# A convolution with two expert layers: folds in pairs, a clamp moved to ScalarE, a spectrum computed earlier, tiles of 512

## The chip, the cores and the metric

The kernel runs on one core of one Trainium2 chip. The metric is the device time of one execution in microseconds. A core has five engines with instruction queues of their own: TensorE multiplies matrices (PE; its weight loads are listed apart as PEld), VectorE (DVE), ScalarE (ACT) and GpSimd (POOL) work element by element, and SyncE (SP) here only issues DMA transfers. ScalarE issues some DMAs too.

## The reference

```python
window = np.exp(-0.01 * np.arange(S))[:, None]                      # S = 12480
h_filt = (np.maximum(pos_emb @ w1, 0) @ w2) * window                # 12480 x 128
u = x * v
y = irfft(rfft(u, 2 * S) * rfft(h_filt, 2 * S), 2 * S)[:S]          # along the sequence
t = x * y                                                           # 12480 tokens x 128
h = t @ moe_w_in;   t = (h * clip(h + 3, 0, 6) / 6) @ moe_w_out     # 128 -> 2048 -> 128
h = t @ moe2_w_in;  out = where(h > 0, h, exp(min(h, 0)) - 1) @ moe2_w_out
```

Everything is fp32, but the four weight matrices of the expert layers arrive as fp64.

## The kernel before, in words

The convolution is a Fourier transform of 196 x 128 points, factored: a first stage of products over 98 rows for each channel, a second over 128 columns for each of 99 frequencies, then back in a third and a fourth. It runs once for the filter and for the signal, and the signal's second stage goes over two halves of 64 channels.

*MLP (`filter_hidden`, L264 to L278).* Eight rounds of eight position products (L267) go to PSUM; VectorE applies relu and window (L271), and the fold (L275 to L278) writes the sum and the difference of two halves to `Rf`. VectorE makes the sums, GpSimd the differences of the first six rounds, VectorE those of the last two. Between rounds stand two calls of `signal` (L254 to L261), three GpSimd operations that make four channels of u = x * v and its own fold. The channel is the outer dimension of `Rf` and the position the inner one, while the data come with the channel inside.

*First stage (L295 to L308).* 32 steps; a step makes eight products (L299; the trace counts two passes of each) for four channels, of the filter or of the signal, and ScalarE copies the result (L302).

*Second stage (`second_all`, L376 to L402).* Its first half goes through 27 groups of up to four frequencies, two groups a turn. For a turn, TensorE makes the filter's spectrum (`second_r`, L324), ScalarE copies it (L327); then come the signal's products (L316) and the filter's last ones (L331). In `second`, ScalarE copies the latter (`ta`, L336), VectorE makes two complex products from them (`tb` and `tc`, L338) and GpSimd combines these (L344). The second half needs no spectrum of its own and goes group by group. The third stage (L353 to L363) stands between the two halves, mixed with the other half's first stage (L420 to L427), and the fourth (L461) makes the tokens.

*Weights (`weight_steps`, L149 to L186).* All through these stages VectorE turns the fp64 weights into fp32 by integer operations, in 32 jobs of 128 x 256 numbers with three steps each. Step one takes the exponent (L174) and the mantissa's upper bits (L175) and clamps the exponent to 896..1151 (L176); step two adds the lower bits (L178), moves the exponent to its place (L179), stores the job before (a DMA on ScalarE's queue, L164) and loads the one after next (SP's queue, L159); step three puts sign and exponent together (L183) and scales (L184). `convert(n)` pays out steps by a rate: 1.1 per step of the first stage, 1.5 per group in the second stage's first half up to frequency 72 (18 groups, so one job in each of nine turns), 1.5 in the third stage, 0.6 per group in the second half.

*Expert layers (L528 to L640).* The tokens go in 26 tiles of `TT` = 480. A tile takes eight units in each of the two layers, and a unit twelve products, six into the hidden layer (L575, `mm1`) and six out of it (L619, `mm2`), since each factor is split into two parts. 26 x 16 x 12 = 4992 products.

No scheduler reorders anything: each engine runs in the order in which the code issues, and the four PSUM buffers of `ps` are shared by all convolution stages.

## Time and profile before

| | us |
|---|---|
| median of three runs | 1441.62 (1440.79 to 1445.14) |
| profiled execution, its own time | 1442.68 |
| its span in the trace | 1440.9 |
| TensorE busy | 1407.4 (98%) |
| VectorE busy | 1235.1 (86%) |
| ScalarE busy | 990.4 (69%) |
| GpSimd busy | 519.8 (36%) |

A span is the time from the first instruction to the last; the execution's own time is 1.8 us longer. The expert layers take 346.00 to 1437.30, three quarters of the span. Busy shares are means over stages that differ, so the rows further down are cut by stage. Where a row ends in square brackets, it says how long the engine had been idle before, and what ended that.

### The profile page before, as it was taken

The numbers are of one execution on the slowest core, as the hardware profiler recorded it, in microseconds if no ns is written. First come the engines' busy times: TensorE is split into PE (matmuls) and PEld (weight loads), VectorE is DVE, ScalarE is ACT, GpSimd is POOL, SyncE is SP. The second block draws the span as 40 slices with busy tenths as digits, with TensorE's granted clock in tenths as the row PEclk, the third lists the DMA queues.
The fourth block names the chain that finished last, engine by engine and source line by source line (L and its number), as shares of the span: only waits on it lengthen the run. The fifth ranks groups of instructions, "written<-read, shape, count | busy, mean of one in ns | idle before, by whom it ended". The sixth has DMA issues, their size and how long they took to land.

```text
span 1440.9 us, 21903 instructions
## 1 busy us (share of the span) xinstructions
PE 1407.4 (98%) x8414; PEld 1229.8 (85%) x8414; DVE 1235.1 (86%) x1401; ACT 990.4 (69%) x1168; POOL 519.8 (36%) x438
## 2 busy tenths in 40 slices
PE   7999999999999999999999999999999999999998
PEld 5888879898888888888888888888888888888887
DVE  7999669788898888888888888888888888888887
ACT  0533332356887877777777777777777777787776
POOL 7855987411332222222222222222222222222223
PEclk9999999999999999999999999999999999999999
DMA  5854355136000000000000000000000000000000
GB/s 186 260 162 139 95 164 150 46 102 182 1 1 7 8 7 7 8 8 0 8 7 7 8 8 7 1 8 7 8 7 8 8 7 1 8 8 8 8 7 14
DMA packets 36660, 60.74 MB, mean 42 GB/s; under 512 B 4290, under 2 KB 17996, under 8 KB 36428
## 3 DMA queue, kind: packets, MB, share of 16 engines
q1 hardware_dynamic: 31436, 54.68, 12.5%
q10 hardware_dynamic: 5120, 4.66, 1.0%
q8 instruction: 66, 1.08, 0.3%
q14 instruction: 38, 0.31, 0.1%
HBM read 48.74 MB, written 10.58 MB: 41 GB/s over the span
## 4 chain that ended last, share of the span: by engine, by line
PE 80%; DVE 12%; POOL 3%; issue 2%; ACT 1%; DMA 1%; SPq 0%; DVEq 0%; POOLq 0%; ACTq 0%
PE h L575 37%; PE o L619 37%; PE y L461 3%; PE q L353 3%; DVE tb L338 2%; DVE tc L338 1%; DVE qb L178 1%; POOL au L344 1%; DVE qb L176 1%; POOL late L260 1%; DVE qb L183 1%; DVE qb L276 1%; POOL ld L257 1%; DVE qb L179 1%; DVE qb L174 1%
## 5 line engine op out<-in xcount | busy, mean ns | idle before, releaser
L619 PE MATMUL o<-gs,w 128*128 128x480 f32 x2496 | 579.5, 380 | 0.2 <-DVE gs L609 0.2
L588 POOL TENSOR_SCALAR a<-a 128x960 f32<-128x960 f32 x208 | 288.1, 1385 | 743.9 <-ACT a L587 703.1
L619 PEld LDWEIGHTS o<-gs,w 128*128 128x128 f32 x2496 | 469.2, 188 | 74.6 <-DVE gs L609 0.6
L609 DVE TENSOR_TENSOR gs<-g,gs 128x960 fp32r<-128x960 f32 x416 | 485.7, 1168 | 4.4 <-ACT gs L604 4.4
L604 ACT CAST gs<-g 128x960 fp32r<-128x960 f32 x416 | 412.6, 992 | 56.4 <-DVE g L596 54.7
L596 DVE SCALAR_TENSOR_TENSOR g<-a,h 128x960 f32<-128x960 f32 x208 | 240.0, 1154 | 140.4 <-ACT a L585 140.3
L575 PE MATMUL h<-xs,w 128*128 128x480 f32 x1248 | 306.2, 381 | 3.0 <-POOL w L490 1.9
L575 PE MATMUL h<-x,w 128*128 128x480 f32 x1248 | 304.1, 379 | 0.0
L575 PEld LDWEIGHTS h<-xs,w 128*128 128x128 f32 x1248 | 234.9, 189 | 40.6 <-POOL w L490 2.3
L587 ACT ACTIVATE a<-h 128x960 f32<-128x960 f32 x208 | 202.4, 973 | 94.4 <-PE h L575 93.5
L575 PEld LDWEIGHTS h<-x,w 128*128 128x128 f32 x1248 | 234.1, 188 | 38.2 <-issue 0.4
L585 ACT ACTIVATE a<-h,three 128x960 f32<-128x960 f32 x208 | 220.9, 1062 | 63.2 <-PE h L575 62.8
L598 DVE SCALAR_TENSOR_TENSOR g<-a,h 128x960 f32<-128x960 f32 x208 | 238.5, 1147 | 0.2 <-POOL a L588 0.2
L344 POOL TENSOR_TENSOR au<-tb,tc 128x256 f32<-128x256 f32 (+3 forms) x108 | 90.2, 868 | 45.4 <-DVE tc L338 44.2
L336 ACT COPY ta<-z 128x512 f32<-128x512 f32 (+3 forms) x54 | 29.7, 550 | 62.1 <-DVE tc L338 25.8
L353 PEld LDWEIGHTS q<-cs,au 128*99 128x99 f32 x512 | 56.6, 170 | 7.2 <-issue 4.6
L353 PE MATMUL q<-cs,au 128*99 128x128 f32 x512 | 60.0, 275 | 2.8 <-POOL au L344 1.8
L490 POOL TENSOR_TENSOR w<-w 128x512 fp32r<-128x512 f32 x16 | 24.6, 1541 | 103.7 <-ACT w L489 60.7
L331 PE MATMUL z<-qb 128*128 128x128 f32 x396 | 53.3, 283 | 4.2 <-ACT qb L327 4.2
L299 PE MATMUL pa<-t,qb 98*64 98x198 f32 x512 | 51.2, 356 | 6.3 <-POOL qb L259 3.7
L359 DVE TENSOR_TENSOR qb<-q,tb 99x512 f32<-99x512 f32 (+2 forms) x68 | 41.4, 654 | 17.9 <-ACT tb L357 17.7
L299 PEld LDWEIGHTS pa<-t,qb 98*64 98x64 f32 x512 | 40.0, 147 | 17.2 <-POOL qb L259 4.4
(56 smaller groups left out, 967.6 us busy)
## 6 DMA issues: line engine op xcount, KB each, us to landing
ld<-in_xc SPq DMA_DIRECT2D x32, 196.0 KB
qb<-in_vc SPq DMA_DIRECT2D x32, 196.0 KB
out_T<-y SPq DMA_DIRECT2D x26, 240.0 KB
xt<-in_xT SPq DMA_DIRECT2D x31, 195.0 KB
qb<-in_mw SPq DMA_DIRECT2D x22, 256.0 KB
qb<-in_gm SPq DMA_DIRECT2D x22, 256.0 KB
...
```

Of the source, the lines that this page charges most:

```text
L299: nc.tensor.matmul(pa[f * HN:(f + 1) * HN, j, :2 * NK], lhsT=src[:, j, f], rhs=t1[:, f], start=True, stop=True)
L344: nc.gpsimd.tensor_tensor(out=Au[:, slots(hf), k0:k0 + nk, r], in0=m1[:, :, :nk, r], in1=m2[:, :, :nk, 1 - r], op=op)
L353: nc.tensor.matmul(q[:NK, r, j], lhsT=Au[:, s0 + j, :, r], rhs=cs[:, r * N2:(r + 1) * N2], start=True, stop=True)
L575: nc.tensor.matmul(h[:, j, :TT], lhsT=wslice(2 * m - 2, a, 2 * u + j), rhs=x[:, b], start=i == 0, stop=i == 2)
L585: nc.scalar.activation(a, h[:, :, :TT], AF.Relu, bias=three)
L587: nc.scalar.activation(a, h[:, :, :TT], AF.Exp)
L588: nc.gpsimd.tensor_scalar(a, a, 1.0, 0.0, op0=ALU.min, op1=ALU.max)
L596: nc.vector.scalar_tensor_tensor(g, a, 6.0, h[:, :, :TT], op0=ALU.min, op1=ALU.mult)
L598: nc.vector.scalar_tensor_tensor(g, a, -1.0, h[:, :, :TT], op0=ALU.add, op1=ALU.max)
L604: nc.scalar.copy(t[:, 0], g)
L609: nc.vector.tensor_tensor(out=t[:, 1], in0=g, in1=t[:, 0].bitcast(F32), op=ALU.subtract)
L619: nc.tensor.matmul(o[:, :TT], lhsT=wslice(2 * m - 1, a, 2 * u + j), rhs=gs[:, b, j], start=u == 0 and j == 0 and i == 0, stop=u == NU - 1 ...
```

## The change

Four edits, with the line numbers of the changed kernel.

The fold (L283) writes `Rf` with two neighbouring channels innermost, so that an output runs over pairs; the first stage's weights are then read with a stride of two (L308).

The clamp of the exponents leaves VectorE. Two ScalarE activations (L184, L185), both relu with an operand of one number per partition from a small tile `ramps`, do the clamp and the shift of the exponent together: relu(1151 - e) and then relu(255 - that), both scaled by 2^23. They are issued at the start of step two, ahead of that step's store.

`second_all` calls `second_r` one turn ahead: `rows(0)` before the loop, and in each turn the spectrum of the next.

`TT` becomes 512: 24 tiles of 512 tokens and one of 192, so 25 x 192 = 4800 products.

```diff
-TT = 480
-NT = S // TT
+TT = 512
+TILES = [slice(t, min(t + TT, S)) for t in range(0, S, TT)]
+NT = len(TILES)
+WID = [t.stop - t.start for t in TILES]
...
-    Rf = qb[:H1, HP:HP + FO * N2].rearrange("p (f s i) -> p f s i", f=FO, s=2)
+    Rf = qb[:H1, HP:HP + FO * N2].rearrange("p (g s i t) -> p s i g t", s=2, i=HN, t=2)
...
+        ramps = const.tile([128, 2], F32, name="ramps")
+        v.memset(ramps[:, :1], 1151 * 2.0 ** 23)
+        v.memset(ramps[:, 1:], 255 * 2.0 ** 23)
...
             v.tensor_scalar(ri, hi_w, 0xFFFFF, 0x100000, op0=ALU.bitwise_and, op1=ALU.bitwise_or)
-            v.tensor_scalar(ei, ei, 896, 1151, op0=ALU.max, op1=ALU.min)
             yield
+            nc.scalar.activation(e, ei, AF.Relu, bias=ramps[:, :1], scale=-(2.0 ** 23))
+            nc.scalar.activation(ei, e, AF.Relu, bias=ramps[:, 1:], scale=-1.0)
             v.scalar_tensor_tensor(r, lo_w, 2.0 ** -32, ri, op0=ALU.mult, op1=ALU.add)
-            v.tensor_scalar(ei, ei, -896, 2 ** 23, op0=ALU.add, op1=ALU.mult)
             store(k - 1)
             load(k + 2)
...
             e.tensor_tensor(
-                out=Rf[:, :, s, i0:i0 + GI].rearrange("p f i -> p i f"), in0=t[:, :, 0], in1=t[:, :, 1], op=op
+                out=Rf[:, s, i0:i0 + GI], op=op, **{
+                    f"in{x}": t[:, :, x].rearrange("p i (g t) -> p i g t", t=2) for x in range(2)
+                },
             )
...
-        first(Rf[:, c * DC:(c + 1) * DC], Ar[:, c * DC:(c + 1) * DC])
+        first(lambda j, f: Rf[:, f, :, c * DC // 2 + j // 2, j % 2], Ar[:, c * DC:(c + 1) * DC])
...
+        def rows(n):
+            if hf == 0 and n <= TAIL:
+                second_r(n, size(n) if n < TAIL else len(KGROUPS) - TAIL)
+        rows(0)
         while n < len(KGROUPS):
...
+            rows(n + size(n))
             g = [
...
-            if hf == 0 and n <= TAIL:
-                second_r(n, len(g) if n < TAIL else len(KGROUPS) - TAIL)
...
-                    h[:, j, :TT], lhsT=wslice(2 * m - 2, a, 2 * u + j), rhs=x[:, b], start=i == 0, stop=i == 2
+                    h[:, j], lhsT=wslice(2 * m - 2, a, 2 * u + j), rhs=x[:, b], start=i == 0, stop=i == 2
```

ScalarE's order in the second stage's first half, before (L336 copies `ta` for both groups of a turn, L164 stores a converted job, L327 copies the spectrum):

```order
L336 COPY ta<-z 128x512 x2
L164 DMA w_scratch<-qb 128x256
L327 COPY qb<-r 128x1024
L336 COPY ta<-z 128x512 x2
L164 DMA w_scratch<-qb 128x256
```

and the same stretch now (L345 is `ta`, L184 and L185 are the ramps, L170 the store, L336 the spectrum's copy):

```order
L345 COPY ta<-z 128x512 x2
L184 ACTIVATE qb<-qb,ramps 128x256
L185 ACTIVATE qb<-qb,ramps 128x256
L170 DMA w_scratch<-qb 128x256
L336 COPY qb<-r 128x1024
L345 COPY ta<-z 128x512 x2
```

The two ramps stand between the `ta` copies of one turn and the store; the store and the spectrum's copy, now that of the turn after, come behind them.

VectorE's order there, before (L338 makes `tb` and `tc`, L174 to L184 are one job):

```order
L338 TENSOR_TENSOR tb<-z,ta 128x4x64x2
L338 TENSOR_TENSOR tc<-z,ta 128x4x64x2
L174 TENSOR_SCALAR qb<-late 128x256
L175 TENSOR_SCALAR qb<-late 128x256
L176 TENSOR_SCALAR qb<-qb 128x256
L178 SCALAR_TENSOR_TENSOR qb<-late,qb 128x256
L179 TENSOR_SCALAR qb<-qb 128x256
L338 TENSOR_TENSOR tb<-z,ta 128x4x64x2
L338 TENSOR_TENSOR tc<-z,ta 128x4x64x2
L183 SCALAR_TENSOR_TENSOR qb<-late,qb 128x256
```

and now (L347 makes `tb` and `tc`):

```order
L347 TENSOR_TENSOR tb<-z,ta 128x4x64x2
L347 TENSOR_TENSOR tc<-z,ta 128x4x64x2
L180 TENSOR_SCALAR qb<-late 128x256
L181 TENSOR_SCALAR qb<-late 128x256
L186 SCALAR_TENSOR_TENSOR qb<-late,qb 128x256
L347 TENSOR_TENSOR tb<-z,ta 128x4x64x2
L347 TENSOR_TENSOR tc<-z,ta 128x4x64x2
L190 SCALAR_TENSOR_TENSOR qb<-late,qb 128x256
L191 SCALAR_TENSOR_TENSOR qb<-qb 128x256
```

Two operations of the job are gone; the exponent operation, which the ramps read, still stands behind the products of the turn's second group.

TensorE's order at the start of the second stage, before (`r` is the spectrum, `z` the products of L316 and L331; x8 counts products, two passes each):

```order
L299 MATMUL pa<-t_91,qb 64x198 x256
L324 MATMUL r<-qb 128x128 x8
L316 MATMUL z<-au,qb 128x128 x8
L331 MATMUL z<-qb 128x128 x8
L324 MATMUL r<-qb 128x128 x8
```

and now:

```order
L308 MATMUL pa<-t_91,qb 64x198 x256
L333 MATMUL r<-qb 128x128 x16
L325 MATMUL z<-au,qb 128x128 x8
L340 MATMUL z<-qb 128x128 x8
L333 MATMUL r<-qb 128x128 x8
```

Two turns' spectra stand ahead of the first turn's products, and afterwards each turn's products stand behind the spectrum of the next.

## Rows read from the trace of the kernel before

**Rows 1.** The page's chain that ended last, share of the span by engine
```profile
PE 80%; DVE 12%; POOL 3%; issue 2%; ACT 1%; DMA 1%; SPq 0%; DVEq 0%; POOLq 0%; ACTq 0%
```

**Rows 2.** Stretches: us; busy (instructions) per engine, PE to POOL; PEclk, DMA share, GB/s
```profile
32.40:80.60 48.20, 45.85 (x478) 36.84 (x478) 47.17 (x72) 22.90 (x29) 40.13 (x40) 0.93 0.79 233
80.60:160.90 80.30, 73.08 (x628) 70.30 (x627) 68.67 (x132) 30.71 (x45) 50.76 (x60) 1.00 0.41 125
160.90:213.50 52.60, 50.76 (x448) 41.40 (x448) 40.05 (x82) 18.86 (x27) 49.95 (x43) 1.00 0.50 155
213.50:270.50 57.00, 52.66 (x430) 50.67 (x429) 47.30 (x77) 16.11 (x29) 44.01 (x54) 0.97 0.45 130
40.00:60.00 20.00, 20.00 (x240) 16.67 (x236) 19.52 (x31) 10.06 (x13) 15.18 (x17) 1.00 0.99 296
```

**Rows 3.** Timeline of PE, end of the MLP: start, us, instruction, [idle before <-releaser]
```profile
28.99 3.13 PE L299 MATMUL pa<-t,qb 98*64 98x198 f32 x16 [0.81 <-POOL qb L260]
...
32.50 3.90 PE L299 MATMUL pa<-t,qb 98*64 98x198 f32 x22 [0.38 <-DVE qb L276]
```

**Rows 4.** Timeline of DVE, folds of the MLP
```profile
14.46 1.05 DVE L276 TENSOR_TENSOR qb<-au 98x512 f32<-98x512 f32 x1
...
29.55 2.90 DVE L276 TENSOR_TENSOR qb<-au 98x512 f32<-98x512 f32 x2
```

**Rows 5.** Timeline of POOL, folds of the MLP and the second signal
```profile
19.77 5.22 POOL L276 TENSOR_TENSOR qb<-au 98x512 f32<-98x512 f32 x3
24.94 1.26 POOL L257 TENSOR_TENSOR ld<-ld,qb 98x512 f32<-98x512 f32 x1
```

**Rows 6.** Groups by line: xcount | busy us, mean ns | idle before
```profile
L359 DVE TENSOR_TENSOR qb<-q,tb 99x512 f32<-99x512 f32 (+2 forms) x68 | 41.4, 654 | 17.9 <-ACT tb L357 17.7
...
L176 DVE TENSOR_SCALAR qb<-qb 128x256 int32<-128x256 int32 x32 | 22.8, 711 | 0.0
...
L179 DVE TENSOR_SCALAR qb<-qb 128x256 int32<-128x256 int32 x32 | 16.3, 511 | 0.0
```

**Rows 7.** Timeline of DVE, one turn of the second stage's first half
```profile
114.80 0.28 DVE L174 TENSOR_SCALAR qb<-qb 128x256 int32<-128x256 int32 x1
...
117.25 0.68 DVE L338 TENSOR_TENSOR tb<-z,ta 128x512 f32<-128x512 f32 x1
...
120.97 0.28 DVE L174 TENSOR_SCALAR qb<-late 128x256 int32<-128x256 int32 x1
```

**Rows 8.** Timeline of ACT and its DMA queue in that turn
```profile
113.71 0.36 ACTq L164 DMA_DIRECT2D w_scratch<-qb  x1
114.11 1.01 ACT L327 COPY qb<-r 128x1024 f32<-128x1024 f32 x1 [2.38 <-PE z L316]
116.42 0.59 ACT L336 COPY ta<-z 128x512 f32<-128x512 f32 x1 [1.30 <-PE z L331]
```

**Rows 9.** Timeline of PE in that turn
```profile
115.17 2.05 PE L331 MATMUL z<-qb 128*128 128x128 f32 x16 [0.50 <-ACT qb L327]
117.06 1.95 PE L324 MATMUL r<-qb 128*128 128x128 f32 x16
```

**Rows 10.** Groups of ACT by line and shape
```profile
L370 ACT ACTIVATE tmp<-pa,pm 99x196 f32<-99x196 f32 x65 | 26.3, 452 | 16.7 <-DVE ti L371 16.7
...
L336 ACT COPY ta<-z 128x256 f32<-128x256 f32 x4 | 1.5, 372 | 4.5 <-DVE tc L338 4.5
```

**Rows 11.** Timeline of POOL, signals in the third stage
```profile
165.65 0.73 POOL L259 TENSOR_TENSOR late<-ld 98x256 f32<-98x256 f32 x1
...
191.62 2.27 POOL L260 TENSOR_TENSOR late<-ld 98x256 f32<-98x256 f32 x1
```

**Rows 12.** Timeline of DVE, five groups of the second stage's second half
```profile
219.96 0.68 DVE L338 TENSOR_TENSOR tb<-z,ta 128x512 f32<-128x512 f32 x1
...
230.88 0.67 DVE L338 TENSOR_TENSOR tb<-z,ta 128x512 f32<-128x512 f32 x1
```

**Rows 13.** Stretch of the expert layers, PE alone: us, busy (x), PEclk, DMA
```profile
480.00:1408.00 928.00, 928.00 (x4267) 1.00 0.02 7
```

More of the change, by code (lines that the diff above doesn't have):

```diff
@@ L299, in first @@
                 nc.tensor.matmul(
-                    pa[f * HN:(f + 1) * HN, j, :2 * NK], lhsT=src[:, j, f], rhs=t1[:, f], start=True, stop=True
+                    pa[f * HN:(f + 1) * HN, j, :2 * NK], lhsT=src(j, f), rhs=t1[:, f], start=True, stop=True
                 )
@@ L304, in first_u @@
     def first_u(ut, slot):
-        first(ut, Au[:, slot:slot + DC])
+        first(lambda j, f: ut[:, j, f], Au[:, slot:slot + DC])
     def first_r(c):
-        first(Rf[:, c * DC:(c + 1) * DC], Ar[:, c * DC:(c + 1) * DC])
+        first(lambda j, f: Rf[:, f, :, c * DC // 2 + j // 2, j % 2], Ar[:, c * DC:(c + 1) * DC])
     def slots(hf):
@@ L377, in second_all, with size @@
         n = 0
+        def size(n):
+            return min(2 if n == 0 or hf == 0 and n != TAIL - 1 else 1, len(KGROUPS) - n)
+        def rows(n):
+            if hf == 0 and n <= TAIL:
+                second_r(n, size(n) if n < TAIL else len(KGROUPS) - TAIL)
+        rows(0)
         while n < len(KGROUPS):
@@ L381, in second_all @@
                     us.append(signal(*take()))
+            rows(n + size(n))
             g = [
                 (ps.tile([128, 2, KC, 2 * HD], F32, tag="ps", name="z"), take() if hf else gms[(n + i) % len(gms)], *k)
-                for i, k in enumerate(KGROUPS[n:n + (2 if n == 0 or hf == 0 and n != TAIL - 1 else 1)])
+                for i, k in enumerate(KGROUPS[n:n + size(n)])
             ]
-            if hf == 0 and n <= TAIL:
-                second_r(n, len(g) if n < TAIL else len(KGROUPS) - TAIL)
             early = hf == 1 and n == 0
@@ L534, in split @@
         x = xs[t % 2] if m == 1 else sb.tile([128, 2, TT], F32R, tag=f"x{m}", name=f"x{m}", bufs=2)
+        x = x[:, :, :WID[t]]
         nc.scalar.copy(x[:, 0], src)
@@ L542, in load_x @@
         if t < NT:
-            split(n, 1, t, xp[:, t * TT:(t + 1) * TT])
+            split(n, 1, t, xp[:, TILES[t]])
     def leave(n, m, t):
-        y = sb.tile([128, TT], F32, tag=f"y{m}", name=f"y{m}")
+        y = sb.tile([128, TT], F32, tag=f"y{m}", name=f"y{m}")[:, :WID[t]]
         if m == 1:
-            nc.scalar.mul(y, acc[m][:, :TT], 1.0 / 6.0)
+            nc.scalar.mul(y, acc[m][:, :WID[t]], 1.0 / 6.0)
             split(n, 2, t, y)
         else:
-            nc.scalar.copy(y, acc[m][:, :TT])
-            nc.sync.dma_start(outT[:, t * TT:(t + 1) * TT], y)
+            nc.scalar.copy(y, acc[m][:, :WID[t]])
+            nc.sync.dma_start(outT[:, TILES[t]], y)
     units = []
@@ L570, in mm1 @@
         m, t, u = units[n]
-        h = pp.tile([128, 2, 512], F32, tag="h", name="h")
+        h = pp.tile([128, 2, 512], F32, tag="h", name="h")[:, :, :WID[t]]
         x = xin[m, t]
@@ L582, in act1 @@
         h = st[n][0]
-        a = sb.tile([128, 2, TT], F32, tag="a", name="a", bufs=3)
+        a = sb.tile([128, 2, TT], F32, tag="a", name="a", bufs=3)[:, :, :WID[units[n][1]]]
         if m == 1:
-            nc.scalar.activation(a, h[:, :, :TT], AF.Relu, bias=three)
+            nc.scalar.activation(a, h, AF.Relu, bias=three)
         else:
-            nc.scalar.activation(a, h[:, :, :TT], AF.Exp)
+            nc.scalar.activation(a, h, AF.Exp)
             nc.gpsimd.tensor_scalar(a, a, 1.0, 0.0, op0=ALU.min, op1=ALU.max)
@@ L593, in gate @@
         h, a = st[n]
-        g = sb.tile([128, 2, TT], F32, tag="g", name="g", bufs=3)
+        g = sb.tile([128, 2, TT], F32, tag="g", name="g", bufs=3)[:, :, :WID[units[n][1]]]
         if m == 1:
-            nc.vector.scalar_tensor_tensor(g, a, 6.0, h[:, :, :TT], op0=ALU.min, op1=ALU.mult)
+            nc.vector.scalar_tensor_tensor(g, a, 6.0, h, op0=ALU.min, op1=ALU.mult)
         else:
-            nc.vector.scalar_tensor_tensor(g, a, -1.0, h[:, :, :TT], op0=ALU.add, op1=ALU.max)
+            nc.vector.scalar_tensor_tensor(g, a, -1.0, h, op0=ALU.add, op1=ALU.max)
         st[n] = [g]
@@ L602, in hi @@
         g = st[n][0]
-        t = sb.tile([128, 2, 2, TT], F32R, tag="gs", name="gs", bufs=LAG + 1)
+        t = sb.tile([128, 2, 2, TT], F32R, tag="gs", name="gs", bufs=LAG + 1)[:, :, :, :WID[units[n][1]]]
         nc.scalar.copy(t[:, 0], g)
```

2 lines of the change are left out of this document (1 added, 1 removed).

## The prediction

> **What bounds the kernel now.** I read the chain of waits first, since it says which engine's time is the kernel's time: 80% of it is TensorE, 12% VectorE, 3% GpSimd, 1% ScalarE [rows 1]. Those 12% and 3% all lie before the mixture-of-experts layers, so I next cut the span into stages [rows 2]: the filter's MLP up to 32.40 us, the first transform stage to 80.60, the second stage's first half to 160.90, the third stage with the other half's first stage to 213.50, the second stage's second half to 270.50. In the first stage VectorE is busy 47.17 of 48.20 us; in the next TensorE (73.08 of 80.30) and VectorE (68.67) take turns in waiting; in the third GpSimd is the fullest engine besides TensorE, 49.95 of 52.60. The profiled execution took 1442.68 us with a span of 1440.9, 1.06 above the median of 1441.62; sums are made against it, and 1.06 taken off at the end.
>
> **(a) Fold of the MLP.** VectorE's last two folds end at 29.55 + 2.90 = 32.45, and TensorE's first product on the filter, at 32.50, waited only 0.38 for them: until then it worked on the second signal's step, from 28.99 for 3.13, and that waited for GpSimd's signal [rows 3, 4]. So two chains end there, and both must shorten. On VectorE a fold took 1.05 alone, two at the end 2.90, 1.45 each [rows 4]; on GpSimd three in a row 5.22, 1.74 each [rows 5]. A fold writes down a column of strides; after the change its innermost output is two neighbours. The nearest operation that writes such pairs is L359, 512 elements in 654 ns [rows 6]. VectorE's ten folds then save 0.4 to 0.8 each and are done by 26.5 or so. GpSimd has six folds ahead of the second signal; at 1.74 less 0.6 or so, VectorE's own saving halfway, they save 3.6, and the signal's step starts at about 25.3. The step and the wait behind it follow: −3.8. Bounds: −1.2 if GpSimd's fold saves only 0.2, −6 if both chains close up on VectorE's 26.5. The stride of two in the weights of the first-stage products I cost at nothing; TensorE loads weights beside its products, and has 36.84 us of loads in 48.20 [rows 2].
>
> The Trainium skill ("SBUF — State Buffer", section "SBUF: two separate sides") says that VectorE and GpSimd share a port pair under an exclusive lock, which VectorE takes for operations with two inputs in SBUF, and that the other one blocks. The rows agree: 1.45 for a fold beside GpSimd's, 1.05 alone [rows 4]. By it a shorter fold on one engine gives the other its time back too, and (a) would come to −6 and the whole to 1433.5.
>
> **(b) First stage, 48.20 us.** Two operations of a conversion job leave VectorE: the clamp (711 ns) and the exponent's step (511 ns), 1.22 of a job's seven operations; VectorE averages 47.17 / 72 = 0.655, so seven are 4.6 us [rows 2, 6]. They return as two ScalarE ramps, which nothing replaces on VectorE but which the job's last two operations await. A job becomes about 3.9: 3.4 left on VectorE, and about 0.5 of waiting for the ramps that the mantissa's operations don't cover. But TensorE is close behind: in 40 to 60 us it is 20.00 of 20.00 busy, 240 instructions at 16 a step, so 1.33 a step, and the DMA engines are at 0.99 and 296 GB/s [rows 2]. The stage's 72 operations are 10.3 jobs, 40 us for VectorE at 3.9. TensorE's 30 steps on from 32.50 took 1.60 each; at 1.33 they would save 8. As GpSimd (40.13 busy) and the DMA stand close behind I take 1.43, 30 x 0.17 = −5. Bounds: −8 to +6 (the ramps stand behind copies, second rival).
>
> **(c) Second stage, first half: the step that decides.** There are nine turns of two channel groups with one job step each. One turn is 120.97 − 114.80 = 6.17, from exponent operation to exponent operation, and VectorE's products and job operations follow one another in it [rows 7]; over the stage it is 68.67 of 80.30 busy. TensorE waits 0.50 in it for the copy of the filter's spectrum [rows 9]: that wait goes, as the spectrum is now a turn ahead, but it isn't what sets the turn. What does afterwards is the order of ScalarE's queue. Before, a turn is: copy of the second group, store (0.36), spectrum copy (1.01), copy of the next turn's first group (0.59) [rows 8]. Now two ramps stand between that copy and the store, and they wait for the exponent operation, which VectorE reaches only behind the two products of the second group. Everything behind the ramps on ScalarE waits too: the store, the spectrum copy and the next turn's first copy, for which VectorE's next products wait. So a ring: exponent operation 0.28, 0.04 to the ramp, 0.48 + 0.02 + 0.48, 0.04, store 0.36 and 0.04, spectrum copy 1.01, copy 0.59 and 0.03, in all 3.37; then VectorE from its first product at 117.25 to the next exponent operation at 120.97, 3.72 [rows 7]. Less a few hundredths of overlap, 7.0 a turn in place of 6.17: 9 x 0.84 = +7.6.
>
> The ramp's price: 256 elements without an operand per partition took 372 ns, 196 elements with one 452 [rows 10]; the latter at 0.85 ns an element (0.59 for 512 [rows 8], against 372) would be 503 for 256. I take 0.48, nearest to the row with the operand; the ends move a turn by −0.22 and +0.04.
>
> The Trainium skill ("ScalarE: Activation LUTs", section "Rules for kernel authors") says that relu, max, min, add and multiply belong on VectorE, not on ScalarE: it speaks against this edit. By its figure for an activation with an operand per partition (section "What ACT_TABLE_LOAD costs", 280 ns and 0.833 per element) a ramp would be 0.49 and the turn by an estimate 7.02; the trace has no ramp yet to compare.
>
> Ahead of the loop a turn's spectrum is now computed before anything can cover it: 16 more products, 1.95 as in [rows 9], of which the end of the first stage hides a part, +1.2. Together +8.8. Bounds: −4 (first rival) to +10.5 (ramps at 0.5 and nothing of the start hidden). The turns behind the last conversion are unchanged but for the layout of waits; nothing.
>
> **(d) Third stage.** Here GpSimd is fullest, 49.95 of 52.60 with 43 operations [rows 2]. A signal undisturbed is 1.26 + 0.73 + 0.73, and one subtraction took 2.27 in place of 0.73 [rows 5, 11]. Fourteen signals at 2.72 would be 38.1, so 11.8 are stalls; two of the seven VectorE operations of a job that get in GpSimd's way go, 2/7 of that, 3.3; I take −3. Bounds: 0 (TensorE, 50.76 busy, holds the stage) to −4.
>
> **(e) Second stage, second half.** Five groups took 230.88 − 219.96 = 10.92 with one job in them [rows 12]. The two operations that leave (1.22) shorten VectorE's share, and here the ramps wait for nothing, since the exponent operation is two groups earlier. Over 18 groups 18 / 5 x 1.22 = 4.4; TensorE's 52.66 of 57.00 allows 4.3 [rows 2]. I take −4.3; bounds −6 (TensorE's own time is stretched too) to 0.
>
> **(f) Tiles of 512.** 4267 matmuls of 480 columns took 928.00 us, 217.5 ns each at a granted clock of 1.00, that is 2.4 GHz [rows 13]; 480 columns alone are 200, so 17.5 go to something else. If that is fixed, 512 columns take 230.8; if it grows with the columns, 232.0; I take 231.4. There are now 24 wide tiles and one of 192 columns, 192 matmuls each: 4608 x 0.2314 = 1066.3. A narrow matmul: 80 + 17.5 = 97 by the fixed excess, 122 for 128 columns in the convolution [rows 9]; 110 taken, 21.1. In all 1087.4, against 4992 x 0.2175 = 1085.8: +1.6. The last copy is 288 columns shorter, at 0.85 ns −0.2. So +1.4; bounds −3.8 (230.8 and 97) to +6.5 (232.0 and 122). ScalarE's and VectorE's work per column doesn't change.
>
> **Sum.** −3.8 − 5 + 8.8 − 3 − 4.3 + 1.4 = −5.9: 1442.68 − 5.9 − 1.06 = 1435.7.
>
> **Rivals.**
> First: the ring in (c) doesn't close, because VectorE runs the exponent operation early enough or the copies come in time. Then TensorE sets the turn: three runs of 16 products, 1.89 from one's start to the next's [rows 9], are 5.6, 9 x (5.6 − 6.17) + 1.2 = −3.9 in place of +8.8, and the time is 1423. For it: VectorE has 1.22 less in each turn, and TensorE's wait goes. Against: the order on ScalarE's queue is fixed, and each link has a row.
>
> Second, slower: the ramps stall ScalarE also outside (c). In the first stage ScalarE has a copy per step, which waits for that step's products; a ramp behind it is late, and the job's end with it, and the copies behind the ramp are late and hold TensorE's buffers. It decides from a job period of 4.6 us on; at 5.1 the stage loses 5 in place of gaining 5, and in (e) the gain is 0: −5.9 + 10 + 4.3 = +8.4, 1450. For it: ScalarE is already held there by stores that wait for VectorE. Against: ScalarE is busy only 22.90 of 48.20 [rows 2].
>
> Third: a matmul's time in the expert layers isn't set by its columns but by the weights that must be loaded for each, so that 512 columns cost 217.5 as well: 4800 x 0.2175 = 1044.0, −42 in place of +1.4, and 1392. For it: the 17.5 ns over the columns. Against: products of 128 columns with weights of the same size come at 122 ns [rows 9], so loading alone does not take 217.
>
> That the change doesn't do what it says is partly so by (c): the spectrum a turn ahead removes a wait of 0.50 where another engine sets the pace.
>
> **How the numbers follow.** Forecast 0.61, with a range of its own from 1428 to 1443 (a third of it above 1437.3, by (c) at its upper end or (b) at less than its −5); first rival 0.17; second 0.15; third 0.07. What a measurement of this kernel can tell from no change is about 0.3%, 4.3 us: faster is below 1437.3, slower above 1445.9. Faster: 0.61 x 0.66 + 0.17 + 0.07 = 0.64; slower 0.12, the larger part of the second rival; the rest, 0.24, within. The range from 1419 to 1449 holds the forecast, the first rival and part of the second, and leaves out the third.
>
> **What would show it.** In the changed profile: the filter's first L308 product at about 28.7, and the second signal's step at 25.3; folds of 0.65; a turn of 7.0 in the second stage's first half, with VectorE's first product waiting for ScalarE's copy, and that for the spectrum copy behind the ramps; no wait of TensorE for the spectrum copy; five groups of the second half in 9.7; wide matmuls 231 ns apart. Wrong, if turns are below 6.2 (first rival), if jobs in the first stage take over 4.6 (second), or if wide matmuls come below 228 (third).

## The result: 1426.7 us, and the profile after

The changed kernel takes 1426.72 us in the median of four runs (1425.11 to 1427.80); its ratio to the kernel before is 0.9892, with a 95% interval from 0.9870 to 0.9913. It is faster by 1.1%; the forecast of 1435.7 was 0.4% under the median then known. The profiled span is 1425.8 us. TensorE's timeline gives the lengths of the stages in both traces (the first stage from its third step, the first of the filter, to the spectrum's first product; the others from the first product of one to that of the next, or to the last):

| us | third step starts | first stage | second stage, first half | third stage | second stage, second half | expert layers |
|---|---|---|---|---|---|---|
| before | 31.3 | 49.3 | 80.3 | 52.6 | 52.0 | 1091.3 |
| after | 29.7 | 48.5 | 86.2 | 47.9 | 46.2 | 1083.0 |
| forecast's term | −3.8 (a) | −5 (b) | +8.8 (c) | −3 (d) | −4.3 (e) | +1.4 (f, with the end) |
| measured | −1.6 | −0.8 | +5.9 | −4.7 | −5.8 | −8.3 (end −0.6) |

The first four stages in the trace of the changed kernel, as in [rows 2]:

```profile
29.70:78.20 48.50, 45.69 (x483) 35.41 (x479) 41.14 (x59) 33.91 (x52) 40.34 (x40) 0.96 0.84 241
78.20:164.40 86.20, 76.17 (x628) 72.30 (x627) 57.42 (x105) 36.38 (x63) 52.86 (x61) 0.96 0.36 111
164.40:212.40 48.00, 48.00 (x451) 40.17 (x450) 39.51 (x63) 25.98 (x43) 45.25 (x42) 1.00 0.53 163
212.40:258.60 46.20, 45.41 (x396) 44.90 (x396) 38.48 (x65) 18.72 (x34) 38.66 (x45) 1.00 0.57 158
```

VectorE, the third busy figure, is nowhere full now. In the first row it went from 48.37 of 49.40, over the same steps, to 41.14 of 48.50, and the stage hardly got shorter; in the second it waits; in the third TensorE is busy throughout. The first row of before, cut as above:

```profile
31.30:80.70 49.40, 46.77 (x483) 37.10 (x481) 48.37 (x72) 23.37 (x29) 41.23 (x41) 0.92 0.77 228
```

The chain that ended last shows the same, where [rows 1] had 80% TensorE and 12% VectorE:

```profile
PE 86%; DVE 4%; POOL 3%; DMA 3%; issue 2%; ACT 2%; SPq 0%; DVEq 0%; POOLq 0%; ACTq 0%
```

One turn of the second stage's first half. ScalarE, as in [rows 8]:

```profile
115.75 0.51 ACT L184 ACTIVATE qb<-qb,ramps 128x256 f32<-128x256 int32 x1 [3.66 <-DVE qb L180]
116.29 0.51 ACT L185 ACTIVATE qb<-qb,ramps 128x256 int32<-128x256 f32 x1
116.30 0.33 ACTq L170 DMA_DIRECT2D w_scratch<-qb  x1
116.71 0.99 ACT L336 COPY qb<-r 128x1024 f32<-128x1024 f32 x1
117.60 1.07 ACT L345 COPY ta<-z 128x512 f32<-128x512 f32 x2
```

VectorE, as in [rows 7], and TensorE, as in [rows 9]:

```profile
115.44 0.28 DVE L180 TENSOR_SCALAR qb<-qb 128x256 int32<-128x256 int32 x1
...
118.29 0.69 DVE L347 TENSOR_TENSOR tb<-z,ta 128x512 f32<-128x512 f32 x1 [1.39 <-ACT ta L345]
...
122.02 0.28 DVE L180 TENSOR_SCALAR qb<-late 128x256 int32<-128x256 int32 x1
```

```profile
117.75 1.18 PE L325 MATMUL z<-au,qb 128*128 128x128 f32 x8
119.72 1.16 PE L325 MATMUL z<-au,qb 128*128 128x128 f32 x8 [0.79 <-DVE tc L347]
```

The ramps wait 3.66 us for the exponent operation, everything behind them follows without a gap, and VectorE's product waits 1.39 for the copy at the end of that train: the ring, link by link. A turn is 122.02 − 115.44 = 6.58. Counted from one turn's signal products to the next turn's, the first three turns go at 5.40 and the seven behind them at 6.58; before, two took 5.50 and 5.89 and eight 6.16. TensorE no longer waits for the spectrum's copy, but for VectorE. Two of the early turns, 92.64 − 87.24 = 5.40 apart:

```profile
87.24 1.99 PE L325 MATMUL z<-au,qb 128*128 128x128 f32 x16
...
92.64 1.99 PE L325 MATMUL z<-au,qb 128*128 128x128 f32 x16
```

The MLP's folds on GpSimd and its end on TensorE, as in [rows 5] and [rows 3], two folds of VectorE with what GpSimd began beside each, and a stretch of the expert layers, as in [rows 13]:

```profile
19.10 4.68 POOL L283 TENSOR_TENSOR qb<-au 98x512 f32<-98x512 f32 x3
```

```profile
9.73 0.69 DVE L283 TENSOR_TENSOR qb<-au 98x512 f32<-98x512 f32 x1
9.79 1.77 POOL L283 TENSOR_TENSOR qb<-au 98x512 f32<-98x512 f32 x1 [9.34 <-DVE au L278]
...
16.06 1.26 POOL L264 TENSOR_TENSOR ld<-ld,qb 98x512 f32<-98x512 f32 x1
16.13 1.74 DVE L283 TENSOR_TENSOR qb<-au 98x512 f32<-98x512 f32 x1
```

```profile
27.32 8.94 PE L308 MATMUL pa<-t,qb 98*64 98x198 f32 x64 [0.58 <-POOL qb L267]
```

```profile
550.00:1300.00 750.00, 750.00 (x3277) 1.00 0.02 7
```

GpSimd's fold went from 1.74 to 1.56 only; the second signal's products, but for its first two, start at 27.32 where it was 28.99. A product of 512 columns takes 750 / 3277 = 228.9 ns.

### The profile page after: what moved, and what is told of

It is laid out like the page before. It is cut to its first block, busy times and chain, and to the rows that moved or that the text cites. A ratio compares the mean times of both kernels' runs of the same rounds, so it can differ in the third digit from the quotient of the medians.

```text
span 1425.8 us, 21334 instructions
## 1 busy us (share of the span) xinstructions
PE 1395.5 (98%) x8222; PEld 1176.6 (83%) x8222; DVE 1206.4 (85%) x1305; ACT 1010.9 (71%) x1196; POOL 519.1 (36%) x430
## 4 chain that ended last, share of the span: by engine, by line
PE 86%; DVE 4%; POOL 3%; DMA 3%; issue 2%; ACT 2%; SPq 0%; DVEq 0%; POOLq 0%; ACTq 0%
PE o L638 37%; PE h L594 37%; PE q L362 4%; PE pa L308 3%; PE y L479 2%; POOL au L353 1%; PE z L325 1%; PE z L340 1%; DVE tb L347 1%; DVE gs L628 1%; DVE tc L347 1%; POOL ld L264 1%; DMA qb<-in_vc 1%; ACT qb L336 1%; DMA xt<-in_xT 1%
## 5 line engine op out<-in xcount | busy, mean ns | idle before, releaser
L638 PE MATMUL o<-gs,w 128*128 128x512 f32 (+1 forms) x2400 | 574.9, 388 | 0.0
L607 POOL TENSOR_SCALAR a<-a 128x1024 f32<-128x1024 f32 (+1 forms) x200 | 292.9, 1464 | 731.4 <-ACT a L606 689.6
L628 DVE TENSOR_TENSOR gs<-g,gs 128x1024 fp32r<-128x1024 f32 (+1 forms) x400 | 484.5, 1211 | 8.4 <-ACT gs L623 8.4
L623 ACT CAST gs<-g 128x1024 fp32r<-128x1024 f32 (+1 forms) x400 | 408.8, 1024 | 55.9 <-DVE g L615 53.7
L615 DVE SCALAR_TENSOR_TENSOR g<-a,h 128x1024 f32<-128x1024 f32 (+1 forms) x200 | 238.8, 1194 | 131.1 <-ACT a L604 131.1
L594 PE MATMUL h<-xs,w 128*128 128x512 f32 (+1 forms) x1200 | 303.9, 389 | 3.2 <-POOL w L508 2.0
L594 PE MATMUL h<-x,w 128*128 128x512 f32 (+1 forms) x1200 | 299.0, 385 | 0.1
L606 ACT ACTIVATE a<-h 128x1024 f32<-128x1024 f32 (+1 forms) x200 | 201.2, 1006 | 95.2 <-PE h L594 93.7
L604 ACT ACTIVATE a<-h,three 128x1024 f32<-128x1024 f32 (+1 forms) x200 | 219.0, 1095 | 62.5 <-PE h L594 62.2
L617 DVE SCALAR_TENSOR_TENSOR g<-a,h 128x1024 f32<-128x1024 f32 (+1 forms) x200 | 237.4, 1187 | 0.0
L347 DVE TENSOR_TENSOR tb<-z,ta 128x512 f32<-128x512 f32 (+3 forms) x54 | 34.7, 643 | 36.9 <-ACT ta L345 23.7
L345 ACT COPY ta<-z 128x512 f32<-128x512 f32 (+3 forms) x54 | 28.9, 553 | 40.8 <-DVE tc L347 17.8
L308 PE MATMUL pa<-t,qb 98*64 98x198 f32 x512 | 50.2, 349 | 5.4 <-POOL qb L266 3.3
L368 DVE TENSOR_TENSOR qb<-q,tb 99x512 f32<-99x512 f32 (+2 forms) x68 | 41.4, 654 | 14.1 <-ACT tb L366 13.8
L308 PEld LDWEIGHTS pa<-t,qb 98*64 98x64 f32 x512 | 38.4, 144 | 17.0 <-POOL qb L267 4.5
```

What stands on the lines that cost most here:

```text
L308: nc.tensor.matmul(pa[f * HN:(f + 1) * HN, j, :2 * NK], lhsT=src(j, f), rhs=t1[:, f], start=True, stop=True)
L594: nc.tensor.matmul(h[:, j], lhsT=wslice(2 * m - 2, a, 2 * u + j), rhs=x[:, b], start=i == 0, stop=i == 2)
L604: nc.scalar.activation(a, h, AF.Relu, bias=three)
L606: nc.scalar.activation(a, h, AF.Exp)
L607: nc.gpsimd.tensor_scalar(a, a, 1.0, 0.0, op0=ALU.min, op1=ALU.max)
L615: nc.vector.scalar_tensor_tensor(g, a, 6.0, h, op0=ALU.min, op1=ALU.mult)
```

## The experiments

### Which edit brought what

**Tiles of 480 in the changed kernel.**

```diff
-TT = 512
+TT = 480
```

> The changed kernel with tiles of 480 again, all else as changed. Theory W (a product of 512 columns costs 229.1 ns, less than the 231.4 that I took, so the tiles brought most of the gain): the expert layers go back from 1083 to about 1091 us, products 217.5 ns apart, the convolution stays 6 us shorter than before; in all about 1436. Rival (the tiles cost about nothing, as in the prediction's term of +1.4, and the gain lies elsewhere): the time stays at 1425 to 1428.

Measured: 1436.24 us, ratio to before 0.9961 (0.9943 to 0.9978); expert layers 1091.4, products 750 / 3449 = 217.5 ns apart:

```profile
550.00:1300.00 750.00, 750.00 (x3449) 1.00 0.02 7
```

So the tiles are worth about 0.7% of the 1.1%, the three edits of the convolution 0.4%.

**The fold alone, in the kernel before.**

```diff
-    Rf = ...rearrange("p (f s i) -> p f s i", f=FO, s=2)
+    Rf = ...rearrange("p (g s i t) -> p s i g t", s=2, i=HN, t=2)
-                out=Rf[:, :, s, i0:i0 + GI].rearrange("p f i -> p i f"), ...
+                out=Rf[:, s, i0:i0 + GI], ...
-        first(Rf[:, c * DC:(c + 1) * DC], ...
+        first(lambda j, f: Rf[:, f, :, c * DC // 2 + j // 2, j % 2], ...
```

> The kernel before with the fold in pairs of channels alone. Theory F (the fold is all that shortened the stages up to the end of the first one): the first stage ends at about 78, 2.5 to 3 us earlier than the 80.7 of before, later stages keep their length, 1440 or so in all. Rival J (the shorter conversion jobs gave it): the first products on the filter start 2 to 3 us earlier, but the first stage ends at 80 or later, since VectorE's jobs still take 4.6 us each.

Measured: ratio 0.9995 (0.9978 to 1.0013), no difference that can be told. In its trace the third step starts at 28.5 and the first stage still takes 48.7; where the start lies differs by some microseconds from run to run (22.2 to 26.7 for the first product, over the traces of all kernels here). The fold's 1.6 us are not shown by a time, then. What the traces show is the stretch from the first product to the third step: 7.6 to 8.9 us, 8.2 in the mean, in the three kernels with the fold as before, and 5.7 to 8.0, 6.6 in the mean, in the twelve with pairs whose signals are as before. The means differ by 1.6, but the two ranges overlap.

**The clamp back on VectorE, in the changed kernel.**

```diff
+            v.tensor_scalar(ei, ei, 896, 1151, op0=ALU.max, op1=ALU.min)
             yield
-            nc.scalar.activation(e, ei, AF.Relu, bias=ramps[:, :1], scale=-(2.0 ** 23))
-            nc.scalar.activation(ei, e, AF.Relu, bias=ramps[:, 1:], scale=-1.0)
             v.scalar_tensor_tensor(r, lo_w, 2.0 ** -32, ri, op0=ALU.mult, op1=ALU.add)
+            v.tensor_scalar(ei, ei, -896, 2 ** 23, op0=ALU.add, op1=ALU.mult)
```

> The changed kernel with the clamp and the exponent's step on VectorE as before; fold, spectrum ahead and tiles of 512 as changed. Theory: first stage unchanged within 1 us (it isn't VectorE that holds it), turns of the second stage's first half at 6.2 in place of 6.58 (-3.5), third stage +4 to +5, second stage's second half +5 to +6; in all 1432 to 1434. Rival (VectorE's jobs hold the first stage too, as the prediction said): 5 us more in the first stage, in all 1437 to 1439.

Measured: 1431.95, ratio 0.9924 (0.9895 to 0.9953). First stage 49.9, second stage's first half 81.8 with turns of 6.17, third 53.4, second half 50.4. So between these two traces the ramps gain 5.5 us in the third stage and 4.2 in the second half, lose 4.4 where the ring is, and bring 1.5 or less in the first stage. The 5.5 is not sure: the kernel with the fold alone, which has the clamp on VectorE too, takes 49.4 in its third stage, 1.5 above the changed kernel.

### What holds the first stage

**No clamp and no exponent's step at all, in the kernel before.**

```diff
-            v.tensor_scalar(ei, ei, 896, 1151, op0=ALU.max, op1=ALU.min)
...
-            v.tensor_scalar(ei, ei, -896, 2 ** 23, op0=ALU.add, op1=ALU.mult)
```

> The kernel before with the clamp and the exponent's step left out altogether (the weights it makes are then not the reference's), nothing put on ScalarE for them. Theory S (signals, not VectorE, hold the first stage): from its 33rd product to its end 48 to 49 us as with everything so far, though VectorE has a quarter less to do. Rival V (VectorE's jobs hold it, as the prediction had it): 43 to 45. In the second stage's first half the turn falls from 6.17 to 5.4 to 5.9, for there is no ring without ramps.

**No product x * v in the first stage's signals, in the changed kernel.**

```diff
-        nc.gpsimd.tensor_tensor(out=xt, in0=xt, in1=vts[n % 3], op=ALU.mult)
+        if n >= NC:
+            nc.gpsimd.tensor_tensor(out=xt, in0=xt, in1=vts[n % 3], op=ALU.mult)
```

> The changed kernel without GpSimd's product x * v in the signals of the first stage (so those signals are of x alone); the loads of v stay. Theory S (a signal of 1.26 + 0.73 + 0.73 us and its wait for v set the later half of the first stage, one signal per two steps of 1.34): the first stage from its 33rd product on falls from 48.5 to 44 us or less, as its later steps go to 1.34. Rival D (the DMA transfers, at 0.86 busy, hold it, or ScalarE behind its ramps): 47 to 49.

Measured (one run each, 1433.54 and 1417.67 us), first stage of the kernel without the two operations:

```profile
34.30:82.90 48.60, 45.87 (x483) 36.66 (x482) 40.89 (x57) 23.93 (x31) 40.13 (x41) 0.93 0.83 239
```

and of the one without the product:

```profile
27.20:68.70 41.50, 40.96 (x481) 35.48 (x481) 29.00 (x55) 33.03 (x52) 20.79 (x26) 1.00 0.94 275
```

With 40.89 of 48.60 in place of 48.37 of 49.40 for VectorE the stage stays as it was. With GpSimd at half it falls to 41.5, which is 1.34 a step nearly throughout, TensorE's own pace, with the DMA engines busier than ever. So the signals hold this stage: GpSimd's three operations, with their waits for v. Leaving the product out takes away a third of the operations and the wait for v together; which of the two counts is not shown by it. In the changed kernel GpSimd waits 5.2 us for v's loads in this stage.

The clock is a rival that these rows raise: it is 1.00 without the product, and in the others it was 0.50, that is 1.2 GHz, for a part of the stage (before from 29.1 to 39.3, after from 27.1 to 33.9). It does not make the 7 us, for with the fold alone it was 1.00 throughout, and the stage took 48.7:

```profile
29.10:39.30 10.20, 9.82 (x58) 6.80 (x60) 10.06 (x15) 2.53 (x3) 9.96 (x8) 0.50 0.50 132
```

```profile
28.45:77.19 48.74, 42.55 (x480) 36.62 (x480) 46.88 (x71) 22.56 (x29) 41.74 (x41) 1.00 0.82 234
```

The first of these is the kernel before, the second the one with the fold alone. There the first three steps of the stage took 0.9 us over 1.34 each, where they took 4.4 before, and the later ones 7.6 in place of 4.7: the time won at the start went into waits later. In the changed kernel the last third of the steps shows it, in the timeline of TensorE:

```profile
60.84 3.02 PE L308 MATMUL pa<-t,qb 98*64 98x198 f32 x32 [0.32 <-POOL qb L267]
64.18 2.91 PE L308 MATMUL pa<-t,qb 98*64 98x198 f32 x32 [0.32 <-POOL qb L267]
```

**A signal's subtraction on VectorE** (first stage, 14 signals; in the kernel of the next part that does best).

```diff
-        nc.gpsimd.tensor_tensor(out=ut[:, :, 1], ...
+        (nc.vector if 2 <= n < NC else nc.gpsimd).tensor_tensor(out=ut[:, :, 1], ...
```

> The kernel with the shifted conversion step and the spectrum in its own turn, and in 14 of the first stage's 16 signals the subtraction on VectorE in place of GpSimd. Theory S (GpSimd's three operations a signal, 2.72 us and more against two steps of 2.68, hold the first stage's later half): GpSimd needs 2.0 a signal, the first stage falls by 3 to 5 us, the kernel to 1410 to 1412. Rival D (the DMA transfers hold it, or VectorE, which in its fixed order now also waits for signals, becomes the bound): no gain or a loss, 1414 to 1420.

Measured: 1413.26, ratio 0.9808 (0.9787 to 0.9829), against 0.9815 (0.9783 to 0.9846) without it: not told apart. The first stage takes 47.2 in place of 48.1; the 3 to 5 us of theory S did not come. VectorE now waits for GpSimd's product in its fixed order, and GpSimd once for a load of x (3.0 us). GpSimd's other two operations also got longer, in the mean from 1.37 to 1.56 and from 0.80 to 1.07 us, so its busy time fell by 5.8 only. That GpSimd's work alone is the bound is thus not shown; that the stage waits for the signals is.

### What sets a turn of the second stage's first half

**One conversion step earlier.**

```diff
+    convert(1)
     second_all(0)
+    due[0] -= 1
```

> The changed kernel with one conversion step more paid ahead of the second stage's first half and one less behind it, so that in each of the nine turns the exponent operation stands one group earlier than the ramps that read it. Theory R (the turn of 6.58 us is a ring through ramps, store, spectrum copy and the next copy): the ramps wait for nothing, the turn falls to 5.6 to 5.8, where TensorE's three runs of 16 products set it, and the kernel to 1418 to 1421. Rival V (VectorE's or GpSimd's own work sets the turn): the turn stays at 6.4 to 6.6 and the time at 1426.

Measured: 1416.14, ratio 0.9828 (0.9807 to 0.9849), better than either kernel. Its turn on ScalarE and TensorE:

```profile
108.35 0.58 ACT L345 COPY ta<-z 128x512 f32<-128x512 f32 x1 [0.31 <-PE z L340]
109.67 0.51 ACT L184 ACTIVATE qb<-qb,ramps 128x256 f32<-128x256 int32 x1 [0.73 <-DVE qb L180]
110.21 0.51 ACT L185 ACTIVATE qb<-qb,ramps 128x256 int32<-128x256 f32 x1
110.22 0.33 ACTq L170 DMA_DIRECT2D w_scratch<-qb  x1
110.63 0.99 ACT L336 COPY qb<-r 128x1024 f32<-128x1024 f32 x1
112.86 0.58 ACT L345 COPY ta<-z 128x512 f32<-128x512 f32 x1 [1.24 <-PE z L340]
```

```profile
108.15 1.95 PE L333 MATMUL r<-qb 128*128 128x128 f32 x16
109.94 1.99 PE L325 MATMUL z<-au,qb 128*128 128x128 f32 x16
111.77 1.95 PE L340 MATMUL z<-qb 128*128 128x128 f32 x16
113.55 1.95 PE L333 MATMUL r<-qb 128*128 128x128 f32 x16
```

The copies now wait for TensorE, TensorE for nothing; the turn is 113.55 − 108.15 = 5.40, three runs of 1.8. The stage takes 74.6, 11.6 less than in the changed kernel and 5.7 less than before. Turn and time came out below what theory R said (5.6 to 5.8, 1418 to 1421). The ramps still wait 0.73, which costs nothing where they stand: the expectation that they wait for nothing was wrong in that.

**The same, with the spectrum in its own turn again.**

```diff
-        rows(0)
...
-            rows(n + size(n))
             g = [
...
             ]
+            rows(n)
```

> The kernel with the shifted conversion step and the filter's spectrum computed in its own turn again, as before. Theory (once TensorE sets the turn, a wait for the spectrum's copy is its price, and without the ring that is the only use of the spectrum one turn ahead): the turn goes from 5.40 to 5.7 to 5.9 us, nine turns and three without conversion lose 3 to 5 us, but about 2 us come back at the start of the stage; 1417 to 1420. Rival (the wait is hidden behind VectorE): 5.40 still, and the kernel 2 us faster than with the spectrum ahead, 1414.

Measured: 1414.49, ratio 0.9815 (0.9783 to 0.9846); turns of 5.41, the stage 73.0. The rival held: without the ring TensorE does not wait for the spectrum's copy in its own turn either, and the spectrum one turn ahead only costs its start, 74.6 − 73.0 = 1.6. The changed kernel with the clamp on VectorE says the same: 81.8 against 80.3 before.

**The kernel without clamp and exponent's step, again.** Its turn fell to 6.02 only, where I expected 5.4 to 5.9. On VectorE, ScalarE and TensorE:

```profile
113.93 0.95 DVE L182 SCALAR_TENSOR_TENSOR qb<-qb 128x256 f32<-128x256 f32 x1
...
118.29 0.69 DVE L336 TENSOR_TENSOR tb<-z,ta 128x512 f32<-128x512 f32 x1 [0.81 <-ACT ta L334]
```

```profile
114.92 0.33 ACTq L164 DMA_DIRECT2D w_scratch<-qb  x1
115.29 1.01 ACT L325 COPY qb<-r 128x1024 f32<-128x1024 f32 x1 [2.23 <-PE z L314]
117.60 0.59 ACT L334 COPY ta<-z 128x512 f32<-128x512 f32 x1 [1.30 <-PE z L329]
```

```profile
112.22 1.95 PE L322 MATMUL r<-qb 128*128 128x128 f32 x16
```

The scaling of a job ends at 114.88, its store goes out at 114.92, and the spectrum's copy, though its data were there 1.1 us earlier (112.22 + 1.95 = 114.17), only behind it; then come TensorE's products, `ta`, and VectorE's next products. That is a ring as well, through the store. So:

```diff
-            store(k - 1)
+            store(k - 2)
```

> The kernel before with the clamp and the exponent's step left out (its weights are then not the reference's) and each job stored two jobs later in place of one. Without the two operations alone the turn only fell from 6.17 to 6.02 us. Theory Q (that turn too is a ring: VectorE's last operation of a job, the store that waits for it on ScalarE's queue, the spectrum copy behind it, TensorE's products, the copy that VectorE's products wait for): with a store that waits for nothing the turn is 5.4 to 5.6. Rival V (VectorE's or GpSimd's work sets it): 6.0 still.

Measured: turns of 5.40, the stage 73.2, the kernel 1428.05 (one run). With a store of an older job, which is ready, the ring is gone. The kernel before had the same order, and its store at 119.88 went out as the job's scaling ended (118.89 + 0.96):

```profile
118.89 0.96 DVE L184 SCALAR_TENSOR_TENSOR qb<-qb 128x256 f32<-128x256 f32 x1
...
119.88 0.35 ACTq L164 DMA_DIRECT2D w_scratch<-qb  x1
```

So the same chain ran through its turn, in which VectorE was full as well. Which of the two set its 6.17 is not shown: no run moves the store alone in that kernel.

### What a product of the expert layers costs

Products in 750 us from 550 to 1300, with the width and the layout changed in the changed kernel. First the width (448, and 496, 416 and 384 in the same line):

```diff
-TT = 512
+TT = 448
```

> The changed kernel with tiles of 448 (27 and one of 384), for the time of a product by its columns. 480 columns took 217.5 ns, 17.5 more than 480 columns at 2.4 GHz; 512 took 229.0, 15.7 more. Theory E (the excess falls with the columns, as weight loads of 188 ns leave less slack in a shorter product): 448 columns at 205 to 207 ns, an excess of 19 or so. Rival F (a fixed excess of 16 to 17): 203. Rival G (the width is not the cause, 512 is special): 17.5 or a little less, 204.

> The changed kernel with tiles of 496 (25 and one of 80), buffers laid out at 496. If the excess over 2.4 GHz is 15.7 at widths that are whole multiples of 64 and larger elsewhere, a product takes 224 to 225 ns (206.7 + 17.5 or a little more); if 480 alone is odd, 222.4.

The moving operand's buffers at 512 numbers a row, with 480 used:

```diff
-        x = xs[t % 2] if m == 1 else sb.tile([128, 2, TT], F32R, ...
+        x = xs[t % 2] if m == 1 else sb.tile([128, 2, 512], F32R, ...
```

> The changed kernel with tiles of 480, but the buffers of the moving operand (x of both layers and the split gate) laid out at 512 numbers a row, so that every 480 columns begin where 512 did. By width so far: 448 columns 202.5 ns, 15.8 over 2.4 GHz; 480 217.5, 17.5 over; 512 229.0, 15.7 over. Theory A (where a row begins makes the 1.8 ns): 215.7 to 216, the expert layers 1082 to 1084 us. Rival W (480 columns themselves, 7.5 times 64, make it): 217.5 and 1091.

All buffers so:

```diff
-        a = sb.tile([128, 2, TT], F32, tag="a", ...
+        a = sb.tile([128, 2, 512], F32, tag="a", ...
```

> The changed kernel with tiles of 480 and every buffer of the expert layers laid out at 512 numbers a row, so that the weights and all buffers lie where they do with tiles of 512. Theory W (a width of 7.5 times 64 costs the rest): 216.9 ns a product, as with the moving operand alone padded, 16.9 over 2.4 GHz. Rival L (where the buffers lie makes it): 215.7 ns, the excess of 448 and 512.

> The changed kernel with tiles of 416 (6.5 times 64). Theory W (whole multiples of 64 have an excess of 15.7 to 15.9 ns over 2.4 GHz, others 17.5): 173.3 + 17.5 = 190.9 ns a product. Rival (the excess differs without such a pattern): 189 ns, or the weight load of 188 ns shows and the product takes 200 or more.

> The changed kernel with tiles of 384 (6 times 64). Theory W: 160.0 + 15.8 = 175.8 ns a product. Rival P (the weight load of 188 ns, listed beside each product, is a floor): 188 ns or more.

| columns | products in 750 us | ns each | over the columns at 2.4 GHz | expert layers, us |
|---|---|---|---|---|
| 384 | 4309 | 174.1 | 14.1 | 1097.8 |
| 416 | 3958 | 189.5 | 16.2 | 1097.0 |
| 448 | 3705 | 202.4 | 15.8 | 1089.3 |
| 480 | 3449 | 217.5 | 17.5 | 1091.4 |
| 480, operand padded | 3459 | 216.8 | 16.8 | 1087.2 |
| 480, all padded | 3460 | 216.8 | 16.8 | 1088.4 |
| 496 | 3345 | 224.2 | 17.5 | 1106.1 |
| 512 | 3277 | 228.9 | 15.5 | 1083.0 |

The 384-column row in the trace:

```profile
550.00:1300.00 750.00, 750.00 (x4309) 1.00 0.02 7
```

The excess is smaller at the three whole multiples of 64 (14.1 to 15.8) than at the three others (16.2 to 17.5). Between 448 and 416 that is 0.4 only, and six widths with one trace each are no rule. Theory E, that the excess grows as the columns get fewer, failed at 448. Where rows begin makes 0.6 to 0.7 of the 1.9 between 480 and 512; the rest stays with the padded buffers, so it goes with the width. My numbers for 384 and 416 were 1.4 to 1.7 ns too high. What in the engine makes the excess stays open. The last column compares less well than the others: in the traces of 480, 480 all padded, 496 and 512 the granted clock was 0.50 for 3.4 us at the start of the layers, and with tiles of 512 and without that the layers took 1081.5 (clamp on VectorE), 1.5 less.

That weight loads of 188 ns set a floor is refuted: products of 384 columns come every 174. But below that there is a floor, as the narrow tile of the changed kernel shows:

```profile
1416.47 0.83 PE L594 MATMUL h<-x,w 128*128 128x192 f32 x6
1417.14 0.83 PE L638 MATMUL o<-gs,w 128*128 128x192 f32 x6
```

From start to start, six products of 192 columns take 0.67 us, 112 ns each. Products of 128 columns in the turns of 5.40 come 1.79 / 16 = 112 ns apart, and those of 80 columns with tiles of 496 also 112. What sets it was not tested.

## Why the prediction was wrong

The first thing that failed is **(f)**, "if that is fixed, 512 columns take 230.8; if it grows with the columns, 232.0". From one width I carried the excess of 17.5 on in two ways and took these for both ends. It is neither: at 512 it is 15.5, less than at 480, and no run shows the growth or the fixed excess that I assumed. 4608 x (0.2289 − 0.2314) = −11.5 against the term. The narrow product: of the 1083.0 us, 1054.8 are wide products and 5.5 the start and end that 1091.3 − 1085.8 left before, so 22.7 / 192 = 118 ns with the waits between them, where I took 110, +1.5. In a row they come 112 ns apart, and so do products of 128 columns: the 122 that I read for these is the length of a run of 16 by 16, with the whole of its last product in it. The end of the kernel fell by 0.6 where I had 0.2. Expert layers and end together: −8.9 in place of +1.4. This difference of 10.3 is more than the whole miss between the two profiles, 15.1 − 5.9 = 9.2; my bound for this term was −3.8.

**(b)** failed as a mechanism. "VectorE is busy 47.17 of 48.20 us" was read as the bound, and TensorE's mean of 1.60 a step as slack that VectorE takes. The two leave-out kernels show otherwise: 15% less on VectorE changes nothing, a GpSimd operation less, with its wait for v, takes 7 us. The steps had to be looked at one by one. Fourteen of the 32 already went at 1.34 before, and the excess lies in the first five (4.4 down to 2.2) and in the later ones that wait for a signal. In the early ones the granted clock was 0.50, from 29.1 to 39.3, after TensorE had waited 2.88 and 0.81 us for GpSimd; [rows 2] has this as a mean of 0.93, and I passed over it. A full engine in the row of a stage is no bound if nothing waits for it.

**(a)** had the two chains right and GpSimd's saving wrong. VectorE's shortest folds came to 0.69 (0.65 forecast), but GpSimd's fold fell by 0.18 where I took 0.6, which is the bound that I gave as −1.2. Two readings were wrong. The 1.05 before was not a fold alone: GpSimd's fold began 0.04 behind it. VectorE's folds that begin just ahead of GpSimd take 1.05 before and 0.69 now, and those that begin just behind it 2.06 and 1.74. And 32.50 was the filter's second product; the first began at 31.3. GpSimd's folds, before (L276) and now (L283):

```profile
9.98 2.02 POOL L276 TENSOR_TENSOR qb<-au 98x512 f32<-98x512 f32 x1 [9.54 <-DVE au L271]
...
21.77 1.28 POOL L276 TENSOR_TENSOR qb<-au 98x512 f32<-98x512 f32 x1
```

```profile
20.83 1.27 POOL L283 TENSOR_TENSOR qb<-au 98x512 f32<-98x512 f32 x1
```

A fold of GpSimd that begins ahead of VectorE's takes 1.28 before and 1.27 now, so the layout gave GpSimd nothing of its own. One that begins behind VectorE's went from 2.02 to 1.77, as VectorE's got shorter by 0.36. So GpSimd's saving was VectorE's, handed on in part; the layout's gain on one engine was not to be carried over to the other.

**(c)** was right in place and mechanism: the ring closed, and its links are those that I listed. Its size was off: 6.58 a turn, not 7.0, and seven such turns, not nine. VectorE's part was 3.73 as read; the way from the exponent operation to VectorE's next product took 2.85 (115.44 to 118.29), not 3.37. The links overlapped: the store went out beside the second ramp, the copies began 0.1 before the one ahead had ended. Ramps cost 0.51, not 0.48. The first ten turns made +1.5 in place of +7.6, since the first three go at 5.40; the start made +1.5, where I had 1.2. The other +2.9 of the stage's +5.9 came behind these turns, which I had put at nothing. The granted clock fell to 0.50 (1.2 GHz) there, in a wait of TensorE of 3.30 us for VectorE:

```profile
156.80:163.60 6.80, 6.03 (x34) 4.69 (x36) 4.91 (x13) 1.83 (x4) 6.80 (x12) 0.50 0.08 29
```

In five other traces with the same turns the clock was low for 3.4 us there and not 6.8, and the stage took 85.4 to 85.5, so by an estimate from these about 1.4 of the 2.9 is the clock's. The first rival, that the ring does not close, is refuted for the changed kernel, though its time of 1423 lay nearer to the result; its three runs of 1.89 are 5.67, not 5.6, and without the ring they came to 5.40. I also missed that a chain through the store stood in the kernel before: without two of VectorE's operations the turn fell to 6.02 only, and with the store moved too to 5.40. That VectorE's operations follow one another in the turn was true and not the whole reason.

**(d)** and **(e)** went as forecast and somewhat further, −4.7 and −5.8. With ramps, or without the two operations, the third stage takes 47.5 to 48.3 and the second half 46.1 to 46.2 in every trace; with the clamp on VectorE 49.4 to 53.4 and 50.4 to 52.0. What makes the third stage differ by 4 us among the latter stays open, so (d) is shown in its direction and not in its size. In (e) the 52.0 of before goes with the clock, 0.50 from 213.4 to 216.8; the two other kernels with the clamp on VectorE, at 1.00, take 50.4. So the ramps made 4.2 of the −5.8, close to the forecast, and the rest goes with the clock. The stretch in the kernel before, and in the one with the fold alone:

```profile
213.51:265.52 52.01, 48.89 (x397) 47.09 (x396) 44.47 (x70) 15.04 (x26) 39.03 (x45) 0.97 0.46 134
```

```profile
207.21:257.63 50.42, 47.45 (x398) 45.63 (x396) 45.68 (x76) 15.04 (x26) 38.98 (x45) 1.00 0.51 145
```

TensorE's 52.66 busy of 57.00, from which I took the limit of 4.3, was no floor: that stretch runs 5 us past the stage, and for the same work TensorE's busy time is 47.45 here and 45.41 in the changed kernel, both at 1.00.

The terms of the convolution came to −7.3 and measured −6.3 at the start of the expert layers (0.7 of the stages' −7.0 came back in the fourth), by errors that cancel: −8.8 against −2.5 up to the end of the first stage, +8.8 against +5.9 in the stage with the ring. The second rival, stalls of ScalarE elsewhere, is refuted by the first stage and by (e); the third by the widths. On the Trainium skill's rule that relu and the like belong on VectorE ("ScalarE: Activation LUTs", "Rules for kernel authors"): here the ramps gained in two stages, lost in one by where they stood, and with one step moved no stage is longer than before. The Trainium skill's price for an activation with an operand per partition ("ScalarE: Activation LUTs", "What ACT_TABLE_LOAD costs"), 0.49 by the estimate, agrees with 0.51 measured. On the port that by the Trainium skill VectorE and GpSimd share ("SBUF — State Buffer", "SBUF: two separate sides"): that each engine's fold takes longer behind the other's than ahead of it agrees, and so does that GpSimd got back some of what VectorE saved; but the estimate of −6 did not come, as two folds in a row beside GpSimd still took 2.32 to 2.88.
